# A causal mask as a bank-opening product, and sixteen fp32r warming products, in an mLSTM and feed-forward kernel

## The chip, the cores and the metric

The kernel runs on one core of a Trainium2 chip. The metric is the device time of one execution in microseconds (us), smaller is better. The engines are named as in the profile: PE is TensorE's matrix multiplications and PEld its weight loads, DVE is VectorE, ACT is ScalarE, POOL is GpSimd, and SP issues most of the DMAs.

## The reference

Two layers follow each other. The first is an mLSTM with 4 batches of 8 heads, 768 steps and a head dimension of 40; the second is a feed-forward layer on 3072 tokens (320 to 2048 to 320) with a leaky activation whose slope differs by channel.

```python
for t in range(S):
    m_new = max(f[t] + m, i[t])
    C = exp(f[t] + m - m_new) * C + exp(i[t] - m_new) * outer(v[t], k[t])
    n = exp(f[t] + m - m_new) * n + exp(i[t] - m_new) * k[t]
    y[t] = sigmoid(o[t]) * (C @ q[t]) / max(abs(n . q[t]), 1)
    m = m_new
x = y as (tokens, heads * dim)
h = x @ w_in
out = (max(h, 0) + alpha * min(h, 0)) @ w_out
```

## The kernel before

**Chunks.** The recurrence is computed in chunks of 128 steps, six to a batch, 24 in all, each with all 8 heads. For a chunk `n` and a parity `par` (four heads of even or of odd number), the scores `pS` are products of keys and queries in one PSUM bank of 128 x 512. They are multiplied by a decay matrix `E`: row `s`, column `t` holds exp(L[t] + b[s]), where `L` is the running sum of the log forget gates and `b` a bias of each source step. `E` must be zero where `t < s`; that is the causal mask.

**How `E` is made.** For chunks 0 to 3 PE spreads the row `L` over 128 partitions into a bank `pb`, by four products of 128 columns (one a head): in `spread` for chunks 0 and 1 (L898), in `stage_b` for 2 and 3 (L419), where `LP` holds the sums in three bf16 parts. For later chunks a DMA brings the spread rows (`Lb`). ScalarE takes the exponential with `b` as its bias (L909, L425). Then GpSimd's `affine_select` writes zeros where `t < s` (L913, L429). VectorE multiplies scores and `E` (L933, L447), and PE multiplies the result with the values (`pH`, L311).

**The feed-forward layer.** Tokens are taken in 12 groups of 256 (two chunks). Each operand is split into a high and a low part in fp32r, so that the first layer has 8 products of 256 columns for each of 16 blocks (L593 to L600) and the second 6 of 320 columns (L623). Weights come as 64-bit words; ScalarE and VectorE convert and split them during the first 100 us (L696, L708, L710, L718, L722). Group 1 starts while group 0 is still running.

**What sets the order.** The start, up to the transposed tokens of group 0, is pinned: each name in the string `ORDER` is a step, emitted in that order, and on every engine each instruction is chained to the one before. `sp`, `ex`, `ms`, `sc` and `wg` with a chunk and a parity are the spread, the exponential, the mask, the scores and their multiplication; `l3a` to `l3e` split the sums of chunk 1; `lf`, `li`, `bj`, `wt`, `wd` are gate arithmetic; `u0m` and `u0c` are the state's products and copy; `warmN` are N products of 256 bf16 columns into an unused bank `o0`, which keep PE running. After it the scheduler places instructions by its own estimates, as far as dependences allow. `FILL` gives warming products ahead of the values of chunks 3 to 5. Banks for attention alternate between two tags (`psa`).

Of the kernel before, what the change touches and what calls it, by code (L numbers as in the profile page):

```python
# [17 lines left out]
def kernel(ctx: ExitStack, tc: tile.TileContext, q, k, v, i_gate, f_gate, o_gate, w_in, w_out, alpha, out):  # L18
    nc = tc.nc
    B, H, S, D = q.shape  # L20
    DM, DFF = w_in.shape
    P = 128
    BH = B * H
    NC = S // P
    NPR = H // 2
    GC = 2
# [15 lines left out]
    def psa(name):  # L42
        turns.reverse()
        return ps_a.tile([P, 512], F32, tag=turns[0], name=name)
# [40 lines left out]

    LP = const.tile([3 * BH, GT], BF16, tag="LP", name="LP")
    pick = const.tile([3 * BH, BH], BF16, tag="pick", name="pick")

    def load_qk(n):
        b, c = divmod(n, NC)  # L90
# [317 lines left out]
    def stage_b(n):  # L408

        b, c = divmod(n, NC)  # L410
        Lb, (Q, K, qf) = pre.pop(n), chunk.pop(n)
        Es = []
        for par in range(2):
            E = sb.tile([P, 512], F32, tag="E", name=f"E{n}_{par}", bufs=4)
            if Lb is None:
                pb = psa(f"pb{n}_{par}")
                for p in range(NPR):
                    h = 2 * p + par
                    nc.tensor.matmul(  # L419
                        pb[:, p * P : (p + 1) * P], pick[:, h : h + 1].broadcast_to([3 * BH, P]),  # L420
                        LP[:, n % GC * P : (n % GC + 1) * P], start=True, stop=True,
                    )
            for p in range(NPR):
                h = 2 * p + par
                nc.scalar.activation(  # L425
                    E[:, p * P : (p + 1) * P], Lb[:, h] if Lb is not None else pb[:, p * P : (p + 1) * P], AF.Exp,
                    bias=bT[:, c, b * H + h : b * H + h + 1],
                )
            nc.gpsimd.affine_select(  # L429
                out=E, in_=E, pattern=[[0, NPR], [1, P]], base=0, channel_multiplier=-1,  # L430
                compare_op=ALU.is_ge, fill=0.0,
            )
            if c == 0 and par == 1:
                open_gate(b)
            pS = psa(f"pS{n}_{par}")
            for p in range(NPR):
                sl = slice(p * P, (p + 1) * P)
                if n >= NDIR:
                    h = 2 * p + par
                    for s in range(2):  # L440
                        nc.tensor.matmul(  # L441
                            pS[:, sl], K[: 3 * D, s, h], Q[: 3 * D, s, h], start=s == 0, stop=s == 1
                        )
                else:
                    nc.tensor.matmul(pS[:, sl], K[:R, par, sl], qf[:R, sl], start=True, stop=True)
            if n < NBF:
                nc.vector.tensor_tensor(E, pS, E, ALU.mult)  # L447
                Es.append(E)
            else:
                if par == 0:  # L450
                    E3 = late_pool.tile([P, 2, 512], BF16, tag="t", name=f"E3_{n}", bufs=3)
                Es.append(score_parts(pS, E, E3[:, par]))
            yield
        if c > 0:
            *_, T = from_state(n, qf, Q)
        hv = values(n, Es) if n < NBF else values_by_parts(n, Es)
        if c > 0:
            nc.vector.tensor_tensor(T, T, hv, ALU.add)
            hv = T
# [60 lines left out]
    def attention(n0):  # L520
# [44 lines left out]
    V0, V1 = 0, 2  # L565
    FILL = {3: 4, 4: 14, 5: 4}
    ORDER = """dq0 dq1 dw0 dw2 warm24 dv0 dw1 dw4 do1 dw3 do2 scan lf0a lf0b li0 lf0z L0 bj0 qT0 qc0 kT0 kc0 warm12 sp00
        bTt bTc l3a l3b alT l3c l3d warm6 wt0 ex00 sc00 l3e ms00 warm3 sp01 ewj ex01 ms01 sc01 warm3 eeL wg00 wTt eTt
        wTc eTc lf1a lf1b warm3 w0s wg01 sp10 alC ex10 ms10 warm3 sp11 ex11 qT1 w1s kT1 kc1 w0j0 warm4 li1 wd0 w0j1 w2s
        warm12 u0m qc1 u0c v0 w0h w0l w1j0 L1 w2j0 warm2 sc10 w1j1 warm2 w2j1 wd1 wg10 fsm fst sc11 ms11 warm6 dv1 dq3 wg11 og1  # L570
        lpa lpb bj1 dq2 dL dx2 w1h g0r dx0 g0g lpc lpd lpe g0x g0p w1l dx1 v1 x0 warm4 tadd g1r g1g s0a w2h g1x g1p w2l warm12 x1
        s1a s1d warm3 s0d og2"""

# [237 lines left out]
    def first_group():  # L811
# [17 lines left out]
        w = [None] * 5  # L829
# [2 lines left out]


        make_identity(nc, ident)
        for j in range(NQ):
            nc.gpsimd.memset(qn_t[j][:, :, D:], 0.0)
            nc.gpsimd.memset(kn_t[j][:, :, D:], 0.0)
# [51 lines left out]
        def spread(n, par):  # L889

            pb = psa(f"pb{n}_{par}")
            for p in range(NPR):
                h = 2 * p + par
                if n == 0:
                    pick, x = ident[:BH, h : h + 1].broadcast_to([BH, P]), L
                else:
                    pick, x = row[:, h : h + 1].broadcast_to([3 * BH, P]), L3
                nc.tensor.matmul(  # L898
                    pb[:, p * P : (p + 1) * P], pick, x[:, n * P : (n + 1) * P], start=True, stop=True
                )  # L900
            rows[n, par] = pb

# [2 lines left out]
        def decay(n, par):  # L905
            e = sb.tile([P, 512], F32, tag="E", name=f"E{n}_{par}", bufs=4)
            for p in range(NPR):
                h = 2 * p + par
                nc.scalar.activation(  # L909
                    e[:, p * P : (p + 1) * P], rows[n, par][:, p * P : (p + 1) * P], AF.Exp, bias=bT[:, n, h : h + 1]  # L910
                )
            yield
            nc.gpsimd.affine_select(  # L913
                out=e, in_=e, pattern=[[0, NPR], [1, P]], base=0, channel_multiplier=-1,
                compare_op=ALU.is_ge, fill=0.0,
            )
            E[n, par] = e
            yield

# [20 lines left out]
                p2.append(psa("p2_0"))  # L940
            x_by_channel(0, n, p1[0], p2[0])

        junk = ps_o.tile([P, DM], F32, tag="o0", name="warm")

        def warm(n=1):
            dense(junk, n)
# [129 lines left out]
        for n in range(2):  # L1076
            add(f"qT{n} qc{n}", by_channel(n, 0, nc.scalar.copy))
            add(f"kT{n} kc{n}", by_channel(n, 1, nc.scalar.copy))
            for par in range(2):
                steps[f"sp{n}{par}"] = lambda n=n, par=par: spread(n, par)  # L1080
                add(f"ex{n}{par} ms{n}{par}", decay(n, par))
                steps[f"sc{n}{par}"] = lambda n=n, par=par: scores(n, par)
                steps[f"wg{n}{par}"] = lambda n=n, par=par: weigh(n, par)
        for j in range(3):
# [3 lines left out]
            for step in range(2):  # L1088
                steps[f"w{j}j{step}"] = lambda j=j, step=step: w[j].join([step])
        for name in ORDER.split():  # L1090
            if name.startswith("warm"):
                warm(int(name[4:]))
            else:
                steps[name]()
# [113 lines left out]
```

## Time and profile before

| | |
|---|---|
| time, three runs | 497.78 us median, 497.69 to 501.44 |
| span of the profiled execution | 497.0 us (first to last instruction; its own time is not given apart from the runs) |
| busy: PE, VectorE, ScalarE, GpSimd | 479.6, 324.1, 321.4, 305.9 us |
| mean granted clock of TensorE | 0.997 |
| GpSimd's selects, L429 | 44, mean 677 ns |
| GpSimd's selects, L913 | 4, mean 811 ns |
| warming products, L137 | 107, mean 306 ns |

The span is the time of one execution from its first to its last instruction; some 0.7 us lie around it if it is like the lowest run. In the tables of stretches of time, the columns after the length are busy time (and instructions) of PE, PEld, DVE, ACT and POOL, then the granted clock, the share of busy DMA engines and GB/s. In a timeline, a row is its start, its length, the engine, the line, the operation, output and inputs, shapes and count; what stands in brackets is how long the engine sat idle before it, and what it waited for. [...]

### The profile page before, as it was taken

The numbers are of one execution on the slowest core, as the hardware profiler recorded it, in microseconds if no ns is written. First come the engines' busy times: TensorE is split into PE (matmuls) and PEld (weight loads), VectorE is DVE, ScalarE is ACT, GpSimd is POOL, SyncE is SP. The second block draws the span as 40 slices with busy tenths as digits, with TensorE's granted clock in tenths as the row PEclk, the third lists the DMA queues.
The fourth block names the chain that finished last, engine by engine and source line by source line (L and its number), as shares of the span: only waits on it lengthen the run. The fifth ranks groups of instructions, "written<-read, shape, count | busy, mean of one in ns | idle before, by whom it ended". The sixth has DMA issues, their size and how long they took to land.

```text
span 497.0 us, 11890 instructions
## 1 busy us (share of the span) xinstructions
PE 479.6 (97%) x4509; PEld 458.3 (92%) x4509; DVE 324.1 (65%) x676; ACT 321.4 (65%) x700; POOL 305.9 (62%) x393
## 2 busy tenths in 40 slices
PE   8998889999999999999999999999999999999997
PEld 7877879899998999999899999989999999999997
DVE  7889899945668675675495576666586675642321
ACT  3869498555687776776975677677886663343332
POOL 6542163405559989849498789758888855243242
PEclk9999998999999999999999999999999999999999
DMA  9998977354685577587566675667664230000000
GB/s 171 232 167 235 248 192 216 94 94 96 150 183 118 125 171 160 105 191 151 111 148 131 147 134 123 157 166 139 134 171 76 46 90 1 1 28 1 26 1 26
DMA packets 173922, 61.60 MB, mean 124 GB/s; under 512 B 140154, under 2 KB 166122, under 8 KB 173866
## 3 DMA queue, kind: packets, MB, share of 16 engines
q1 hardware_dynamic: 173786, 60.75, 54.9%
q8 instruction: 35, 0.57, 0.5%
q14 instruction: 21, 0.17, 0.1%
q10 hardware_dynamic: 80, 0.11, 0.1%
HBM read 36.90 MB, written 4.03 MB: 82 GB/s over the span
## 4 chain that ended last, share of the span: by engine, by line
PE 64%; DVE 10%; ACT 8%; POOL 6%; DMA 5%; issue 5%; SPq 1%; ACTq 0%; DVEq 0%; POOLq 0%
PE po L623 25%; PE ph L593 4%; PE ph L596 3%; PE ph L594 3%; PE ph L597 3%; PE ph L599 3%; PE ph L595 3%; PE ph L600 3%; PE ph L598 3%; PE pH L347 2%; PE pS L441 2%; POOL gl L615 2%; PE warm L137 2%; DMA kS<-Z 2%; DMA qS<-Z 1%
## 5 line engine op out<-in xcount | busy, mean ns | idle before, releaser
L615 POOL TENSOR_TENSOR gl<-g,gh 128x512 fp32r<-128x512 f32 x80 | 102.8, 1286 | 62.0 <-ACT gh L614 54.7
L606 DVE SCALAR_TENSOR_TENSOR g<-g,oma,ph 128x256 f32<-128x256 f32 x160 | 69.8, 477 | 74.4 <-ACT g L602 68.8
L623 PE MATMUL po<-OH,gh 128*128 128x320 f32 x368 | 111.1, 314 | 0.6 <-ACT gh L614 0.6
L623 PE MATMUL po<-OL,gh 128*128 128x320 f32 x368 | 109.4, 310 | 0.0
L602 ACT ACTIVATE g<-ph 128x512 f32<-128x512 f32 x96 | 57.1, 595 | 41.0 <-PE ph L600 29.1
L614 ACT CAST gh<-g 128x512 fp32r<-128x512 f32 x80 | 49.5, 619 | 34.4 <-DVE g L606 33.0
L623 PE MATMUL po<-OH,gl 128*128 128x320 f32 x368 | 71.1, 315 | 0.2 <-POOL gl L615 0.2
L623 PEld LDWEIGHTS po<-OH,gh 128*128 128x128 f32 x368 | 69.0, 188 | 1.0 <-ACT gh L614 0.8
L623 PEld LDWEIGHTS po<-OL,gh 128*128 128x128 f32 x368 | 69.0, 188 | 0.0
L593 PE MATMUL ph<-XH,WH 128*128 128x256 f32 x192 | 58.1, 303 | 1.8 <-DVE g L606 0.8
L623 PEld LDWEIGHTS po<-OH,gl 128*128 128x128 f32 x368 | 56.8, 188 | 0.4 <-POOL gl L615 0.4
L425 ACT ACTIVATE E<-Lb,bT 128x128 f32<-128x128 f32 x160 | 51.0, 393 | 7.2 <-PE pH L347 7.1
L429 POOL TENSOR_SCALAR_AFFINE_SELECT E<-E 128x512 f32<-128x512 f32 x44 | 29.8, 677 | 40.7 <-ACT E L425 37.7
L597 PE MATMUL ph<-X,W 128*128 128x256 f32 x192 | 54.5, 285 | 0.0
L594 PE MATMUL ph<-XH,WH 128*128 128x256 f32 x192 | 54.3, 283 | 0.0
L596 PE MATMUL ph<-XH,WL 128*128 128x256 f32 x192 | 54.1, 282 | 0.0
L600 PE MATMUL ph<-X2L,W 128*128 128x256 f32 x192 | 54.0, 282 | 0.0
L599 PE MATMUL ph<-XL,WH 128*128 128x256 f32 x192 | 53.9, 281 | 0.0
L595 PE MATMUL ph<-XH,WL 128*128 128x256 f32 x192 | 53.7, 280 | 0.0
L598 PE MATMUL ph<-XL,WH 128*128 128x256 f32 x192 | 53.5, 279 | 0.0
L334 ACT CAST E<-pS 128x512 bf16<-128x512 f32 x72 | 41.8, 585 | 12.8 <-DVE pS L332 9.0
L593 PEld LDWEIGHTS ph<-XH,WH 128*128 128x128 f32 x192 | 36.2, 188 | 2.9 <-issue 1.0
(199 smaller groups left out, 1154.6 us busy)
## 6 DMA issues: line engine op xcount, KB each, us to landing
Lb<-L_d SPq DMA_DIRECT2D x20, 512.0 KB
wo<-in_moe_w_out_dram SPq DMA_DIRECT2D x8, 640.0 KB
wi<-in_moe_w_in_dram SPq DMA_DIRECT2D x8, 512.0 KB
qn<-in_q_dram SPq DMA_DIRECT2D x24, 160.0 KB
kn<-in_k_dram SPq DMA_DIRECT2D x24, 160.0 KB
va<-in_v_dram SPq DMA_DIRECT2D x24, 160.0 KB
og<-in_o_gate_dram SPq DMA_DIRECT2D x24, 160.0 KB
out_dram<-ob SPq DMA_DIRECT2D x11, 320.0 KB
```

What stands on the lines that cost most here:

```text
L593: nc.tensor.matmul(dst, WH[half][:, 0, hs], XH[:, 0], start=True, stop=False)
L594: nc.tensor.matmul(dst, WH[half][:, 1, hs], XH[:, 1], start=False, stop=False)
L595: nc.tensor.matmul(dst, WL[half][:, 0, hs], XH[:, 0], start=False, stop=False)
L596: nc.tensor.matmul(dst, WL[half][:, 1, hs], XH[:, 1], start=False, stop=False)
L597: nc.tensor.matmul(dst, W2[:, fs], X2, start=False, stop=False)
L598: nc.tensor.matmul(dst, WH[half][:, 0, hs], XL[:, 0], start=False, stop=False)
L599: nc.tensor.matmul(dst, WH[half][:, 1, hs], XL[:, 1], start=False, stop=False)
L600: nc.tensor.matmul(dst, W2[:, fs], X2L, start=False, stop=True)
L602: nc.scalar.activation(gt, ph, AF.Relu, scale=-1.0)
L606: nc.vector.scalar_tensor_tensor(out=y[:, e], in0=gt[:, e], scalar=oma[:, f : f + 1], in1=ph[:, e], op0=ALU.mult, op1=ALU.add)
L615: (nc.vector if g < 2 else nc.gpsimd).tensor_tensor(gl, y, gh.bitcast(F32), ALU.subtract)
L623: nc.tensor.matmul(po[j], x[:, e, j * P : (j + 1) * P], W[f // NB][:, f % NB], **ends)
```

## The change

For chunks 0 to 3, a product now opens the bank `pb`: the matrix `later`, 0 where `t >= s` and -2^100 elsewhere, multiplied with an identity in bf16 and repeated for the four heads. The four products of the spread add to it. The exponential of -2^100 is zero, so GpSimd's select is left out for these chunks. `later` is made by GpSimd at the start, by a memset and a select, ahead of the other memsets. In `ORDER` the four `ms` steps go, and one `warm12` becomes `wide`: sixteen fp32r products of 512, 256, 320 and 128 columns, four each, into the unused bank. Their operand is a tile `even` of 128 x 512, which VectorE writes by one cast from the identity at the start.

```diff
+    later = const.tile([P, P], BF16, tag="later", name="later")
+    def barred(pb):
+        one = ident.bitcast(BF16).rearrange("p (c w) -> p c w", w=2)[:, :, 1]
+        nc.tensor.matmul(pb, one, later.unsqueeze(1).broadcast_to([P, NPR, P]), start=True, stop=False)
...
@@ stage_b
                 pb = psa(f"pb{n}_{par}")
+                barred(pb)
                 for p in range(NPR):
...
-                        LP[:, n % GC * P : (n % GC + 1) * P], start=True, stop=True,
+                        LP[:, n % GC * P : (n % GC + 1) * P], start=False, stop=p == NPR - 1,
...
-            nc.gpsimd.affine_select(
-                out=E, in_=E, pattern=[[0, NPR], [1, P]], base=0, channel_multiplier=-1,
-                compare_op=ALU.is_ge, fill=0.0,
-            )
+            if Lb is not None:
+                nc.gpsimd.affine_select(
+                    out=E, in_=E, pattern=[[0, NPR], [1, P]], base=0, channel_multiplier=-1,
+                    compare_op=ALU.is_ge, fill=0.0,
+                )
...
@@ ORDER
-        bTt bTc l3a l3b alT l3c l3d warm6 wt0 ex00 sc00 l3e ms00 warm3 sp01 ewj ex01 ms01 sc01 warm3 eeL wg00 wTt eTt
-        wTc eTc lf1a lf1b warm3 w0s wg01 sp10 alC ex10 ms10 warm3 sp11 ex11 qT1 w1s kT1 kc1 w0j0 warm4 li1 wd0 w0j1 w2s
-        warm12 u0m qc1 u0c v0 w0h w0l w1j0 L1 w2j0 warm2 sc10 w1j1 warm2 w2j1 wd1 wg10 fsm fst sc11 ms11 warm6 dv1 dq3 wg11 og1
+        bTt bTc l3a l3b alT l3c l3d warm6 wt0 ex00 sc00 l3e warm3 sp01 ewj ex01 sc01 warm3 eeL wg00 wTt eTt
+        wTc eTc lf1a lf1b warm3 w0s wg01 sp10 alC ex10 warm3 sp11 ex11 qT1 w1s kT1 kc1 w0j0 warm4 li1 wd0 w0j1 w2s
+        wide u0m qc1 u0c v0 w0h w0l w1j0 L1 w2j0 warm2 sc10 w1j1 warm2 w2j1 wd1 wg10 fsm fst sc11 warm6 dv1 dq3 wg11 og1
...
         make_identity(nc, ident)
+        nc.gpsimd.memset(later, 0.0)
+        nc.gpsimd.affine_select(
+            out=later, in_=later, pattern=[[1, P]], base=0, channel_multiplier=-1, compare_op=ALU.is_ge, fill=-(2.0**100)
+        )
...
@@ spread
             pb = psa(f"pb{n}_{par}")
+            barred(pb)
...
-                    pb[:, p * P : (p + 1) * P], pick, x[:, n * P : (n + 1) * P], start=True, stop=True
+                    pb[:, p * P : (p + 1) * P], pick, x[:, n * P : (n + 1) * P], start=False, stop=p == NPR - 1
...
@@ decay
-            yield
-            nc.gpsimd.affine_select(
-                out=e, in_=e, pattern=[[0, NPR], [1, P]], base=0, channel_multiplier=-1,
-                compare_op=ALU.is_ge, fill=0.0,
-            )
             E[n, par] = e
...
-        junk = ps_o.tile([P, DM], F32, tag="o0", name="warm")
+        junk = ps_o.tile([P, 512], F32, tag="o0", name="warm")
+        even = late_pool.tile([P, 512], F32R, tag="gh", name="even", bufs=3)
+        nc.vector.tensor_copy(even.rearrange("p (a b) -> p a b", b=P), ident.unsqueeze(1).broadcast_to([P, 4, P]))
+
+        def wide():
+            for cols in (512, 256, 320, 128):
+                for _ in range(4):
+                    nc.tensor.matmul(junk[:, :cols], even[:, :P], even[:, :cols], start=True, stop=True)
```

The order of instructions moves at three places on which the prediction rests. The first is PE's queue in the pinned start, from the second spread of chunk 1 (`pb_1`) over its transposed queries and keys (`pqk`) to the first product of the state (`pu`). Before, the two warming rows after `pqk_1` stand sixteen times in a row:

```order
L898 MATMUL pb_1_311<-L_140,row 128x128 x4
L224 MATMUL pqk_0_321<-ident,qn_76 104x128 x4
L224 MATMUL pqk_1_328<-ident,kn_78 104x128 x4
L137 LDWEIGHTS ident
L137 MATMUL warm<-ident 128x256
L167 MATMUL pu_358<-va_79,kd_341 40x42 x8
```

Now the bank-opening product stands ahead of the spread, and the two warming rows stand four times ahead of the wide ones:

```order
L93 LDWEIGHTS ident
L93 MATMUL pb_1_318<-later,ident 128x512
L911 MATMUL pb_1_318<-L_147,row 128x128 x4
L230 MATMUL pqk_0_329<-ident,qn_76 104x128 x4
L230 MATMUL pqk_1_336<-ident,kn_78 104x128 x4
L143 LDWEIGHTS ident
L143 MATMUL warm<-ident 128x256
L958 MATMUL warm<-even 128x512 x4
L958 MATMUL warm<-even 128x256 x4
L958 MATMUL warm<-even 128x320 x4
L958 MATMUL warm<-even 128x128 x4
L173 MATMUL pu_370<-va_79,kd_349 40x42 x8
```

The same kind of pair stands ahead of the other three spreads of chunks 0 and 1, at the head of what the exponentials wait for. The second place is the head of VectorE's queue, before:

```order
L848 CAST row<-ident 32x32 x3
L849 CAST pick<-row 96x32
L973 SCALAR_TENSOR_TENSOR g_WL_95<-g_WH_94 32x768
L976 TENSOR_TENSOR g_lf_138<-g_WH_94,g_WL_95 32x256
L979 TENSOR_TENSOR g_lf_138<-g_lf_138,g_WL_95 32x256
```

and now:

```order
L860 CAST row<-ident 32x32 x3
L861 CAST pick<-row 96x32
L953 CAST even<-ident 128x512
L988 SCALAR_TENSOR_TENSOR g_WL_96<-g_WH_95 32x768
L991 TENSOR_TENSOR g_lf_145<-g_WH_95,g_WL_96 32x256
L994 TENSOR_TENSOR g_lf_145<-g_lf_145,g_WL_96 32x256
```

The cast stands ahead of the scan of the running maximum (the row of 32x768), on which all gate arithmetic rests. The third place is GpSimd's queue in the part that the scheduler places, for chunks 3 to 5. `E_0_735` and `E_1_759` are chunk 3, `E_0_831` and `E_1_913` chunk 4, `E_0_1237` and `E_1_1421` chunk 5; `xn_719` holds the tokens of group 1, of chunk 2 and then of chunk 3. Before:

```order
L429 AFFINE_SELECT E_0_735<-E_0_735 128x512
L401 TENSOR_TENSOR xn_719<-T_707,og_181 128x320
L405 COPY xn_719<-xn_719 128x64
L429 AFFINE_SELECT E_1_759<-E_1_759 128x512
L429 AFFINE_SELECT E_0_831<-E_0_831 128x512
L145 TENSOR_TENSOR kd_1638<-kn_77,wT 128x320
L429 AFFINE_SELECT E_1_913<-E_1_913 128x512
L429 AFFINE_SELECT E_0_1237<-E_0_1237 128x512
L401 TENSOR_TENSOR xn_719<-T_798,og_181 128x320
L429 AFFINE_SELECT E_1_1421<-E_1_1421 128x512
L405 COPY xn_719<-xn_719 128x64
L145 TENSOR_TENSOR kd_1866<-kn_78,wT 128x320
```

Now, with `xn_730`, `E_0_842` and `E_1_924` for chunk 4, `E_0_1248` and `E_1_1432` for chunk 5:

```order
L151 TENSOR_TENSOR kd_1649<-kn_77,wT 128x320
L407 TENSOR_TENSOR xn_730<-T_718,og_188 128x320
L437 AFFINE_SELECT E_0_842<-E_0_842 128x512
L411 COPY xn_730<-xn_730 128x64
L437 AFFINE_SELECT E_1_924<-E_1_924 128x512
L437 AFFINE_SELECT E_0_1248<-E_0_1248 128x512
L437 AFFINE_SELECT E_1_1432<-E_1_1432 128x512
L151 TENSOR_TENSOR kd_1877<-kn_78,wT 128x320
L407 TENSOR_TENSOR xn_730<-T_809,og_188 128x320
```

The selects of chunk 3 are gone, and the second `xn` of group 1 stands behind the second select of chunk 5 and behind the product `kd_1877`, where before it stood ahead of both.

More of the change, by code (lines that the diff above doesn't have):

```diff
@@ L1080, in first_group @@
                 steps[f"sp{n}{par}"] = lambda n=n, par=par: spread(n, par)
-                add(f"ex{n}{par} ms{n}{par}", decay(n, par))
+                add(f"ex{n}{par}", decay(n, par))
                 steps[f"sc{n}{par}"] = lambda n=n, par=par: scores(n, par)
@@ L1090, in first_group @@
         for name in ORDER.split():
-            if name.startswith("warm"):
+            if name == "wide":
+                wide()
+            elif name.startswith("warm"):
                 warm(int(name[4:]))
```

## The prediction

> **What bounds the kernel now.** I read the busy shares first, then the slices.
>
> ```profile
> PE 479.6 (97%) x4509; PEld 458.3 (92%) x4509; DVE 324.1 (65%) x676; ACT 321.4 (65%) x700; POOL 305.9 (62%) x393
> ...
> PE   8998889999999999999999999999999999999997
> ...
> ```
>
> PE is busy 479.6 of 497.0 us, and in every slice. GpSimd, from which the change takes work, is busy 62%. But PE's share also counts warming products and products that only run long, so I asked for the stretches.
>
> ```profile
> 20.00:30.00 10.00, 9.53 (x93) 8.74 (x88) 9.45 (x21) 6.02 (x12) 5.18 (x6) 1.00 1.25 179
> 30.00:40.00 10.00, 9.09 (x89) 7.76 (x87) 8.02 (x20) 8.47 (x16) 2.38 (x3) 1.00 0.70 196
> ...
> 70.00:80.00 10.00, 8.20 (x56) 7.00 (x55) 9.79 (x17) 8.78 (x19) 4.18 (x5) 0.83 0.84 226
> 100.00:150.00 50.00, 48.91 (x429) 47.73 (x428) 28.22 (x58) 31.96 (x64) 20.73 (x31) 1.00 0.61 134
> ```
>
> The first busy column is PE, the third VectorE, the fifth GpSimd. From 20 to 100 us VectorE is nearly full and PE waits now and then; from 100 us PE alone is full. By the built order the queues differ from before only up to about 115 us; from there on they are the same. So the end moves by as much as PE's work at about 115 us moves, and the question is the first 100 us. There I read the chain of work that ended last.
>
> ```profile
> 8.97 1.08 PE pb L898 x8
> ...
> 15.41 0.50 PE pb L898 x4
> ...
> 15.93 1.65 ACT E L909 x6
> ...
> 21.56 0.04 DVE WL L722
> ```
>
> Up to 15.9 us the chain is PE's own queue without a gap; then ScalarE; from 21.6 us VectorE, which converts weights. GpSimd's masks are not in it.
>
> **The change, part by part.**
>
> *The masks that go.* Eight selects leave GpSimd, four of the first two chunks and four of chunks 2 and 3.
>
> ```profile
> 12.65 0.69 DVE L933 TENSOR_TENSOR E<-pS,E 128x512 f32<-128x512 f32 x1 [0.53 <-POOL E L913]
> ...
> 14.96 0.23 DVE L868 COPY wT<-ps_gw 128x64 f32<-128x64 f32 x1 [1.61 <-PE ps_gw L864]
> ...
> 65.47 0.69 DVE L447 TENSOR_TENSOR E<-pS,E 128x512 f32<-128x512 f32 x1 [0.58 <-POOL E L429]
> ```
>
> Only two waits end with a mask. The first, 0.53 us, is followed on VectorE by 1.61 us of waiting for PE: it is worth nothing, PE's queue is late next. The second, 0.58 us, lies in the VectorE-bound part: I count all of it, **-0.6 us**, between 0 and that.
>
> *The bank-opening products.* Eight bf16 products of 512 columns come in, each ahead of four products of a spread. The trace has none of 512 columns; the nearest row is the warming product of 256.
>
> ```profile
> 17.36 1.91 PE L137 MATMUL warm<-ident 128*128 128x256 bf16 x16
> ...
> 19.11 0.58 ACT L276 COPY kf<-pqk 40x512 f32<-40x512 f32 x1
> ...
> 19.70 0.51 PE L167 MATMUL pu<-va,kd 128*40 128x42 f32 x16 [0.43 <-ACT kf L276]
> ```
>
> Sixteen take 1.91 us; less 0.27 for the last one's own length that is 0.109 us each, so 0.22 us for 512 columns; nothing where PE waits anyway, 0.27 at most. The first stands where PE waits for VectorE's sums (next part) and is hidden. The next three lie in PE's gapless queue: 3 x 0.22 = **0.65 us** on PE, and two of them, 0.43, ahead of ScalarE's exponentials. The four of chunks 2 and 3 stand ahead of these waits of PE, which take them in; without that cover they cost 0.9 us.
>
> ```profile
> PE pb L419 <- ACT qf L284: 1.0, 1, 1.0
> PE ph L593 <- DVE gl L615: 0.7, 1, 0.7
> PE pS L445 <- ACT E L425: 0.7, 1, 0.7
> ```
>
> *The wide warming products.* Sixteen fp32r products of 512, 256, 320 and 128 columns replace twelve of the bf16 ones, 12 x 0.109 = 1.31 us. Their paces are in the feed-forward and in the spread of chunk 1.
>
> ```profile
> 487.79 0.28 PE L598 MATMUL ph<-XL,WH 128*128 128x256 f32 x1
> ...
> 488.14 0.32 PE L623 MATMUL po<-OH,gh 128*128 128x320 f32 x1
> ...
> 489.17 0.31 PE L623 MATMUL po<-OL,gh 128*128 128x320 f32 x1
> ```
>
> Three products of 256 columns start from 487.79 to 488.14, one every 0.117 us, and seven of 320 from there to 489.17, one every 0.147. 512 columns are two of 256, 0.233; 128 are 0.125 (the spread at 15.41, four in 0.50), or 0.06 if half the width takes half the time. Four of each: 4 x (0.233 + 0.117 + 0.147 + 0.125) = 2.49 us, at least 2.2. The swap adds **1.18 us**. The product behind them waited 0.43 us for a copy on ScalarE, which is cover for that much.
>
> *The tile of the wide products.* VectorE writes it by one cast, in front of the long scan with which the start begins.
>
> ```profile
> 1.41 3.33 DVE L848 CAST row<-ident 32x32 fp32r<-32x32 f32 x3 [0.48 <-POOL ident masks.py:199]
> 4.77 0.54 DVE L849 CAST pick<-row 96x32 bf16<-96x32 f32 x1
> 4.86 1.74 DVE L973 TENSOR_TENSOR_SCAN g_WL<-g_WH 32x768 f32<-32x768 f32 x1
> ...
> 5.89 0.52 POOL L268 MEMSET kf<- 64x512 f32 x1
> ...
> 8.90 0.96 PEld L898 LDWEIGHTS pb<-g_L,ident 32*128 32x128 f32 x8 [0.21 <-DVE g_L L982]
> ...
> 10.32 0.27 DVE L1006 CAST L<-g_L 32x256 fp32r<-32x256 f32 x1
> ```
>
> A cast of 256 columns takes 0.27 us at 10.3 us, so 512 take 0.5. But beside GpSimd's memsets three casts of 32 columns took 3.33 us, and the one of `pick` 0.54. GpSimd's memsets last until 6.4 us, and later by 0.5 now, since the barrier tile is made ahead of them (as `ident` was, from 0.80 to 1.31 us). So the scan starts between 0.5 and 1.6 us later; I take 1.0. [...]
>
> PE's weight load waited 0.2 us for the sums at 8.90, so the chain moves by 1.0 - 0.2 = 0.8 us (0.3 to 1.4), and the first new product fits into the wait.
>
> *What is late next.* PE reaches the product of 19.70 us 0.8 + 0.65 + 1.18 - 0.43 = 2.2 us later. VectorE copies its result at 20.65 us, behind a slow multiplication:
>
> ```profile
> 16.58 3.02 DVE L145 TENSOR_TENSOR kd<-kn,wT 128x320 f32<-128x320 f32 x1
> ...
> 20.65 0.66 DVE L182 COPY C<-pu 40x168 f32<-40x168 f32 x2
> ...
> 21.56 0.69 DVE L722 TENSOR_TENSOR WL<-t_wi,WH 128x512 fp32r<-128x512 f32 x1 [0.24 <-ACT WH L718]
> ```
>
> If GpSimd's masks of chunk 1 are part of what stretched that multiplication to 3.02 us, it is shorter now, but VectorE then waits for PE. Of the 2.2 us, 0.44 is the copy's slack (the product takes 0.51 and was done at 20.21) and 0.24 the wait at 21.56: **+1.5 us** (0.8 to 2.1) on VectorE where its own full stretch begins. ScalarE, 0.8 + 0.43 late, is earlier than that.
>
> *What moves.* GpSimd's operations on the second half of the gates start right behind the first weights, at about 10 us, beside VectorE's split of the sums; these are needed by PE at 15.4 us and ended at 12.13: 3 us of cover. In the stretch from 45 to 115 us the second token half of group 1 (`xn`) falls behind a mask and a product on GpSimd.
>
> ```profile
> 72.15 1.32 POOL L401 TENSOR_TENSOR xn<-T,og 128x320 f32<-128x320 f32 x1 [1.58 <-DVE og L399]
> 73.43 0.88 POOL L429 TENSOR_SCALAR_AFFINE_SELECT E<-E 128x512 f32<-128x512 f32 x1
> ...
> 74.46 1.30 POOL L145 TENSOR_TENSOR kd<-kn,wT 128x320 f32<-128x320 f32 x1
> ...
> 79.47 0.42 DVE L492 TENSOR_TENSOR X2L<-p,X 128x256 fp32r<-128x256 f32 x1
> ...
> 84.03 0.19 PEld L598 LDWEIGHTS ph<-XL,WH 128*128 128x128 f32 x1
> ```
>
> It would come 0.88 + 1.30 = 2.2 us later. The last piece made from it is done at 79.9 us, and group 1's first product with a low part starts at 84.03: 4 us of cover, so nothing; without it 2.2. SP's queue only exchanges neighbours (a `kn` ahead of a `wo`, an `Lb` ahead of a `wo`, a `va` ahead of an `Lb`).
>
> **Sum:** +1.5 - 0.6 = +0.9 us. The profiled execution spans 497.0 us, and about 0.7 lie around it if it is like the lowest run (497.69); the median is 497.78. So **498.7 us**; by its own terms 498.0 (the start's shift 0.8) to 500.8 (2.1, no mask's wait won, the later bank products uncovered).
>
> **The rivals.**
>
> *The exchanged queues win the waits back.* From 30 to 100 us PE is idle some 7 us (0.91 and 1.80 of them in the two stretches shown), and once its clock is halved:
>
> ```profile
> 72.00:74.00 2.00, 0.85 (x6) 0.49 (x5) 2.00 (x4) 1.95 (x5) 1.85 (x2) 1.00 0.62 92
> ...
> 76.00:78.00 2.00, 2.00 (x12) 1.75 (x11) 1.94 (x4) 1.47 (x3) 0.00 (x0) 0.50 1.11 360
> ```
>
> PE is idle for more than half of 72 to 74 us, and from 75.0 to 78.4 runs at clock 0.50, which costs 1.7 us. If the new order wins half of the idle time, and a third of the halved stretch, the rest of which holds filler, that is 3.5 + 0.6: 498.7 - 4.1 = 494.6. Against it: VectorE is busy 9.79 of 10 there, and its queue holds the same work.
>
> [...]
>
> *The fp32r pace is a state that the wide products set.* The bf16 products start at 256 / 0.109 = 2.35 columns a nanosecond, the fp32r ones at 2.18 in both widths.
>
> ```profile
> L623 PE MATMUL po<-OH,gh 128*128 128x320 f32 x368 | 111.1, 314 | 0.6 <-ACT gh L614 0.6
> ...
> L593 PE MATMUL ph<-XH,WH 128*128 128x256 f32 x192 | 58.1, 303 | 1.8 <-DVE g L606 0.8
> ```
>
> There are three such groups of 368 and eight of 192. If warming in fp32r brought them to the bf16 pace, 1104 products would gain 0.011 us each and 1536 0.008: 24 us, 475. [...] Against the rival: 2640 such products keep PE at this for 400 us, and the pace at their end is still the slow one.
>
> *The change does nothing that can be seen:* every added piece is covered, 497.8.
>
> **Chances.** Forecast 0.60; queues win 0.14 (a quarter of it beyond 1%); half clock 0.10; fp32r pace 0.13; nothing 0.03. One per cent, 5 us, is about what a measurement of this kernel tells from no change. Faster: 0.13 + 0.04 = 0.17. Slower: 0.09 + 0.02 from the forecast's far tail = 0.11. Same: 0.72. The range runs from 493.5, just below the second case, to 502.8, just short of the third; it leaves out the fp32r pace and a few hundredths on each side.
>
> **What would show it.** In the new profile: the scan of 4.86 us starts near 5.9; the first spread's products near 9.8; the sixteen wide products take 2.5 us; the product of 19.70 us starts near 21.9; VectorE's `WL` of 21.56 us near 23; no wait for a mask at 65 us; and the tail, from 115 us to the end, is as long as before. The forecast is wrong if fp32r products step by other than 0.117 and 0.147 us, if clock 0.50 shows up in more or no stretch, or if PE's waits from 30 to 100 us sum to other than 6 to 8 us.

## The result, and the profile after

| | before | after |
|---|---|---|
| median time | 498.06 us (496.94 to 501.44, 10 runs) | 503.95 us (501.09 to 507.85, 10 runs) |
| ratio to before | | 1.0124, 95% interval 1.0101 to 1.0147 |
| span of the profiled execution | 497.0 us | 500.9 us (its time 502.61) |
| mean granted clock over the runs | 0.997 (the 92 runs of before beside the experiments) | 0.989 |

The change costs 1.2%, about 6 us. The forecast was 498.7 us, with a range up to 502.8. Each listed run's time is 1.7 us above its span, so the 0.7 us that the prediction put around the span was 1 us too small: the profiled execution of before took about 498.7, slightly more than its median. Medians, ratios and clocks, here and below, leave out six runs of the experiments that lie over 1.5% above the fastest of their kernel.

The page of after, its first part:

```profile
PE 482.0 (96%) x4521; PEld 461.2 (92%) x4521; DVE 318.7 (64%) x677; ACT 322.3 (64%) x700; POOL 298.8 (60%) x387
```

GpSimd lost 7 us of work and VectorE 5, on engines that are busy for 60 and 64% of the span. The start came out better than forecast, as the timeline of after shows (start, length, engine, line, and in brackets the idle time ahead):

```profile
1.41 0.55 DVE L860 CAST row<-ident 32x32 fp32r<-32x32 f32 x3 [0.49 <-POOL ident masks.py:199]
...
2.08 0.42 DVE L953 CAST even<-ident 128x512 fp32r<-128x512 f32 x1
4.14 1.75 DVE L988 TENSOR_TENSOR_SCAN g_WL<-g_WH 32x768 f32<-32x768 f32 x1 [1.64 <-DMA g_WH<-in_i_gate_dram]
...
16.02 0.48 DVE L151 TENSOR_TENSOR kd<-kn,wT 128x320 f32<-128x320 f32 x1
...
17.87 2.62 PE L958 MATMUL warm<-even 128*128 128x512 f32 x16
20.42 0.51 PE L173 MATMUL pu<-va,kd 128*40 128x42 f32 x16
...
21.68 0.69 DVE L730 TENSOR_TENSOR WL<-t_wi,WH 128x512 fp32r<-128x512 f32 x1
```

The casts are done at 2.5 us and not at 4.9, the scan waits for a DMA instead, and VectorE's `WL` starts 0.12 us later than in before (21.56). At about 100 us PE's feed-forward is 0.2 to 0.7 us ahead of before. Then it loses time at three places, the last two of them far behind the point from which the queues have the order of before. These are the waiting products of before there:

```profile
111.68 0.41 PE L623 MATMUL po<-OH,gg 128*128 128x320 f32 x1 [0.93 <-ACT gg L614]
...
151.29 0.21 PE L347 MATMUL pH<-vb,E 128*128 128x84 bf16 x1 [1.07 <-ACT E L334]
...
330.99 0.36 PE L593 MATMUL ph<-XH,WH 128*128 128x256 f32 x1 [0.83 <-DVE g L606]
```

And these are the ones of after:

```profile
111.94 0.42 PE L631 MATMUL po<-OH,gg 128*128 128x320 f32 x1 [1.88 <-ACT gg L622]
...
151.51 0.21 PE L353 MATMUL pH<-vb,E 128*128 128x126 bf16 x1 [0.92 <-POOL vb L331]
152.80 0.21 PE L353 MATMUL pH<-vb,E 128*128 128x84 bf16 x1 [1.08 <-ACT E L340]
...
333.49 0.55 PE L601 MATMUL ph<-XH,WH 128*128 128x256 f32 x1 [1.99 <-DVE g L614]
```

The waits are longer by 0.95, 0.92 and 1.16 us, and behind the third PE runs at half clock, which it does not do there in before (table of stretches of after; the figure after POOL's busy time is the granted clock):

```profile
330.00:332.00 2.00, 1.50 (x28) 1.16 (x24) 0.00 (x0) 0.88 (x3) 0.85 (x3) 1.00 0.84 268
333.20:336.50 3.30, 3.01 (x14) 3.04 (x15) 2.74 (x9) 1.82 (x5) 3.00 (x5) 0.50 0.77 191
```

PE's work is 0.3 us later than in before at 111.9 us, 1.5 at 152.8, 2.5 at 333.5 and 3.9 behind the half-clock stretch. From there to the end it stays at 3.9, the difference of the two spans. In between, other waits differ by some 0.3 us in all.

**What the three waits have in common.** Each goes back to a transfer that lands late. At 331 us it is a DMA transpose of a chunk's queries (`qS`), which ScalarE's cast of the next chunk waits for (timeline of before, then of after):

```profile
328.62 0.46 ACT L236 CAST Z<-qn 128x320 bf16<-128x320 f32 x1 [1.28 <-DMA qS<-Z]
```

```profile
331.12 0.46 ACT L242 CAST Z<-qn 128x320 bf16<-128x320 f32 x1 [2.43 <-DMA qS<-Z]
```

Its issue to that cast took 3.30 us before and 4.45 after. The list of DMA queues says what lies between. For the whole execution of before, and then of after, it has this line (packets, MB, share) for a program that comes in pieces of 16 KB:

```profile
q8 instruction: 35, 0.57, 0.5%
```

```profile
q8 instruction: 36, 0.59, 0.5%
```

Here is the view of DMAs of after from 327.5 to 331.2 us, 40 slices of 0.09 us:

```profile
GB/s 266 266 222 67 130 174 174 227 213 396 208 111 66 36 30 11 0 0 0 3 8 8 8 11 8 11 8 11 191 291 288 291 291 436 415 332 415 401 401 415
...
q8 instruction: 1, 0.02, 1.6%
...
qS<-Z SPq DMA_TRANSPOSE x1
```

And from 326.2 to 329.9 us in before, around the same transpose:

```profile
GB/s 288 155 155 114 144 191 222 221 230 216 208 199 221 202 210 199 202 236 349 332 330 374 387 387 374 304 387 244 216 376 221 111 89 66 22 22 0 0 0 169
```

By the list of packets, the transpose of after runs from 327.88 to 330.60 us, and one piece of program starts in its middle, at 328.39. The rate falls from 200 to nothing, and the rest of the transpose follows some 1.2 us later. In before the transpose runs from 326.53 to 328.10, without a hole in the rate; the piece starts at 328.90, when it has ended. The output gates' transfer shows the same. From 104.9 to 108.3 us of after, with a piece at 105.2:

```profile
GB/s 215 226 224 421 194 162 134 156 147 164 169 186 181 188 190 194 139 64 55 36 11 11 9 13 15 15 13 15 15 15 15 15 15 15 6 0 0 0 0 0
```

Its last 1.2 us move at 9 to 15 GB/s. I read that as one DMA engine that was held up by the piece and still has its share to move; the views do not tell the engines apart, so that reading is not shown. ScalarE's step for the sigmoid, ahead of the feed-forward's `gg` in its queue, starts with its table load at 108.31 us instead of 106.38. The third piece, at 140.37, lies in a pair of transposes of 139.0 to 142.7 us. ScalarE's next casts wait for these until 143.31, where before they start at 141.80, and its later steps, for which PE waits at 151, are late by as much.

**Why the pieces moved.** On the average 254 to 255 of the trace's instructions of PE lie between two pieces (251 to 252 of them products and weight loads), in every kernel here. That count is why I take the pieces for PE's program. The change adds 8 bank-opening products and 4 warming ones, each with its weight load: 24 instructions. So every piece behind the start is fetched 24 instructions earlier against the work. At the mean pace, 9042 products and weight loads in 500 us, that is an estimated 1.3 us; the piece that starts at 106.57 us in before starts at 105.21 in after.

### The profile page after: what moved, and what is told of

Same layout as the page of the kernel before. It is cut to its first block, busy times and chain, and to the rows that moved or that the text cites. A ratio compares the mean times of both kernels' runs of the same rounds, so it can differ in the third digit from the quotient of the medians.

```text
span 500.9 us, 11912 instructions
## 1 busy us (share of the span) xinstructions
PE 482.0 (96%) x4521; PEld 461.2 (92%) x4521; DVE 318.7 (64%) x677; ACT 322.3 (64%) x700; POOL 298.8 (60%) x387
## 4 chain that ended last, share of the span: by engine, by line
PE 73%; DVE 9%; ACT 6%; DMA 6%; issue 3%; SPq 1%; POOL 1%; ACTq 0%; POOLq 0%; DVEq 0%
PE po L631 29%; PE ph L601 4%; PE ph L605 4%; PE ph L604 4%; PE ph L602 4%; PE ph L607 4%; PE ph L608 4%; PE ph L603 4%; PE ph L606 4%; PE pH L353 3%; PE pS L449 3%; PE warm L143 2%; DMA qS<-Z 2%; DMA wo<-in_moe_w_out_dram 1%; PE pu L173 1%
## 5 line engine op out<-in xcount | busy, mean ns | idle before, releaser
L601 PE MATMUL ph<-XH,WH 128*128 128x256 f32 x192 | 58.3, 304 | 2.2 <-DVE g L614 2.0
L437 POOL TENSOR_SCALAR_AFFINE_SELECT E<-E 128x512 f32<-128x512 f32 x40 | 25.9, 647 | 30.0 <-ACT E L432 25.5
```

What stands on the lines that cost most here:

```text
L601: nc.tensor.matmul(dst, WH[half][:, 0, hs], XH[:, 0], start=True, stop=False)
```

## The experiments

The theories: **A**, the masks' removal gives another order from 45 to 115 us, and that order costs; **B**, the wide products and the longer start cost; **F**, which came up with the first four runs, the place of PE's program fetches costs; **H**, the half-clock stretches make the rest.

### Parts of the change

The first kernel is after with `warm12` in the place of `wide` and no `even`. The second is before with `wide` and `even`. The third and the fourth take the bank-opening products for chunks 0 and 1, or 2 and 3, alone:

```diff
 spread (chunks 0, 1)        third: kept as in after; fourth: as in before
 stage_b (chunks 2, 3)       third: as in before;     fourth: kept as in after
-  ... w2s wide u0m ...
+  ... w2s warm12 u0m ...    first, third and fourth
```

> The whole change except the wide products: twelve bf16 warming products stand in their old place and the tile of their operand is not made. The queues of GpSimd and SP are those of after, word for word; the masks of chunks 0 to 3 are bank-opening products. Theory A (the masks' removal lets the scheduler place the work from 45 to 115 us in another order, above all SP's two values ahead of the output gates, and PE then waits longer at 110, 150 and 331 us): 503 to 505, the waits of PE at 110 and at 331 us stay at 1.9 and 2.0 us. Theory B (the wide fp32r products make the start longer, and all that follows is late): within 1.5 us of before, 497 to 499.5.

> The kernel before with the sixteen wide products and their tile alone; GpSimd masks all chunks as before, and GpSimd, SP and nearly all of ScalarE have the order of before. Theory A: 497 to 500, since the order from 45 to 115 us is the old one (PE's wait at 110 us near 0.9 us, at 331 near 0.8). Theory B: 501 to 504.

> Bank-opening products for chunks 0 and 1 only (the pinned start); chunks 2 and 3 are masked by GpSimd as before, no wide products. Only four selects leave GpSimd, all inside the pinned order; behind the start every queue has the order of before, except some of VectorE's neighbours. Theory A: 497 to 499, the old waits at 110 and 331 us. If the start itself were the cause (theory B in its wider form: the barrier tile, the casts, the bank-opening products at the head): 500 to 504, with the offset against before there by 22 us and kept to the end.

> Bank-opening products for chunks 2 and 3 only; chunks 0 and 1 are masked by GpSimd in the pinned start as before, no wide products. The order of SP, GpSimd and VectorE from 45 to 115 us is close to that of after. Theory A: 502 to 505, with PE's wait at 110 us at 1.5 us or more. Theory B: 497 to 499.5. A third theory (the offset comes from half-clock stretches that fall anywhere, whatever the order): 498 to 503 with the mean clock below 0.994, and no longer wait at 110 us.

| | median us | ratio to before (interval) | instructions of PE more than before |
|---|---|---|---|
| masks without wide products | 504.77 | 1.0122 (1.0096 to 1.0148) | 16 |
| wide products only | 499.65 | 1.0039 (1.0009 to 1.0069) | 8 |
| chunks 0 and 1 only | 498.95 | 1.0015 (0.9994 to 1.0036) | 8 |
| chunks 2 and 3 only | 499.84 | 1.0018 (0.9993 to 1.0044) | 8 |

Theory B falls with the first row: without the wide products the loss is as large. Theory A falls short with the fourth: it has nearly the order of after and loses 1 to 2 us, not 6. (A's longer wait ahead of the feed-forward's second layer is there in its trace, 1.7 us for `gh` at 106.5 us; A's time is not.) The theory of half clock had asked for a mean clock below 0.994 there; it was 0.9955. The two halves of the masks cost 0.15% and 0.18%, neither told from nothing by its interval, and together 1.2%. No theory had forecast that, and it sent me to the traces of DMAs. The waits of PE in the first kernel:

```profile
PE ph L601 <- DVE g L614: 2.6, 2, 2.2
...
PE pH L143 <- DVE E L455: 2.1, 1, 2.1
```

and in the fourth:

```profile
PE pH L354 <- ACT E L341: 2.3, 2, 1.2
PE pH L144 <- DVE E L456: 2.1, 1, 2.1
...
PE ph L602 <- DVE g L615: 0.8, 1, 0.8
```

Both have the new wait of 2.1 us ahead of chunk 4's values. Only the first has the long wait for `g`, 2.2 us at 336 us, and its trace has a piece of program at 331.46 us inside that transpose. But the first kernel does not lose its time where after does. The wait near 110 us that theory A named for it is not there. PE is 3.3 us behind before at 100 us already. Just ahead of that lie waits of 1.6 and 1.3 us, and 10.24 us at half clock (a row of its table of stretches):

```profile
87.60:97.90 10.30, 9.35 (x53) 8.79 (x54) 7.62 (x16) 4.87 (x13) 3.12 (x4) 0.50 0.14 24
```

### The place of the fetches alone

To shift the fetches and nothing else, warming products of the start are joined in pairs to one of 512 columns (2 instructions fewer for each pair), or halved (2 more). The columns that PE passes stay the same, and so does the order on every other engine:

```diff
         def warm(n=1):
+            x = ident.bitcast(BF16)
+            while n >= 2 and merged[0] > 0:
+                nc.tensor.matmul(junk, x[:, :P], x.unsqueeze(1).broadcast_to([P, 2, 2 * P]), start=True, stop=True)
+                merged[0] -= 1
+                n -= 2
             dense(junk, n)
```

> The changed kernel with 8 of its first 24 warming products joined in pairs to four of 512 columns: the same columns, but 4 products and 4 weight loads fewer in PE's program. Theory F (PE's program is fetched in pieces of 16 KB by a DMA that shares the engines of the data; the change put 24 instructions more into PE's queue, so each fetch comes about 1.5 us earlier against the work, and three of them now hit transfers that PE waits for: the output gates at 105, a transpose at 140, one at 328 us): 8 instructions are too few. The fetches come near 105.6, 140.9 and 328.9 us, all three transfers are still hit, PE's waits near 110, 150 and 331 us stay at 1.9, 0.9 and 2.0 us, and the time is that of after, 502.5 to 505. Theory A (the order of the queues alone): 502.5 to 505 as well. It is the control for the next one.

> The same with 32 products joined to sixteen: 32 instructions fewer than after, 8 fewer than before, the order of every other queue that of after. Theory F: the fetches come near 106.8, 141.7 and 329.9 us, behind the three transfers; PE's waits near 110, 150 and 331 us fall to about 0.9, 0 to 0.3 and 0.8 us, no half clock behind 331 us: 4 to 5 us less than after, 498.5 to 500.5. Theory A: as after, 502.5 to 505.

> The same with 64 products joined to thirty-two: 64 instructions fewer than after. Theory F: the fetches come near 108, 142 and 330.3 us, clear of the three transfers by more; 498 to 501. A gain over the kernel with sixteen pairs would speak for the joined products themselves. Theory A: as after, 502.5 to 505.

> The kernel before with 28 of its warming products at the start split into two of 128 columns each: the same columns, 56 instructions more in PE's program, no other queue changed and no mask moved. Theory F: the fetch of 106.57 us comes near 103.8, into the output gates' transfer, that of 141.3 near 139, into a transpose, and that of 328.9 near 326.9, into the transpose of the queries: PE's waits near 110, 150 and 330 us grow by about 1 us each, with a half-clock stretch behind the last: 501 to 503.5. Theory A, and any theory by which the masks or the wide products are the cause: as before, 497.5 to 499.

| | instructions against before | median us | ratio to before (interval) |
|---|---|---|---|
| after, 4 pairs joined | +16 | 503.6 | 1.0128 (1.0088 to 1.0168) |
| after, 16 pairs joined | -8 | 500.29 | 1.0038 (1.0018 to 1.0058) |
| after, 32 pairs joined | -40 | 502.68 | 1.0114 (1.0073 to 1.0156) |
| before, 28 products halved | +56 | 505.94 | 1.0171 (1.0134 to 1.0207) |

In its profiled run, which took 497.29 us and was the fastest of its twelve, the kernel with sixteen pairs has the three waits back at their old length or below:

```profile
109.44 0.41 PE L631 MATMUL po<-OH,gg 128*128 128x320 f32 x1 [0.62 <-ACT gg L622]
...
149.81 0.21 PE L353 MATMUL pH<-vb,E 128*128 128x84 bf16 x1 [1.03 <-ACT E L340]
...
329.56 0.36 PE L601 MATMUL ph<-XH,WH 128*128 128x256 f32 x1 [0.83 <-DVE g L614]
```

The control with four pairs kept two of them in its profile (1.6 us for `gg`, 2.2 for `g`) and the loss. And before itself, its masks untouched, becomes slower by 1.7% when 56 instructions are added that leave PE the same columns to pass:

```profile
114.99 0.42 PE L623 MATMUL po<-OH,gg 128*128 128x320 f32 x1 [1.81 <-ACT gg L614]
...
156.29 0.21 PE L347 MATMUL pH<-vb,E 128*128 128x126 bf16 x1 [0.93 <-POOL vb L325]
157.59 0.21 PE L347 MATMUL pH<-vb,E 128*128 128x84 bf16 x1 [1.08 <-ACT E L334]
...
340.59 0.36 PE L593 MATMUL ph<-XH,WH 128*128 128x256 f32 x1 [1.58 <-DVE g L606]
```

The first three rows are those of after, in a kernel without the change. It lost more than I forecast, since its pieces hit other transfers too: one starts at 55.9 us, ScalarE waits 3.2 us for a weight of the second layer (2.4 in before), PE then 2.2 us for ScalarE's `qf` (1.0 in before), and 6.83 us at half clock follow.

The kernel with 32 pairs missed its forecast of 498 to 501. Its waits for `gg` and `g` are 0.6 and 0.8 us, as forecast, but its pieces lie elsewhere: one at 58.3 us beside a weight (PE waits 1.5 us for `qf`), one at 136.3 in a pair of transposes (1.4 us for `XH`), and its profile, the slowest of its five runs (507.17 us), is at half clock twice between 62 and 90 us, for 10.24 us each time. These shifts did not end the hits, they exchanged them.

### Both kernels at both places

> The kernel before with 12 of its first warming products split into two of 128 columns each: 24 instructions more in PE's queue, as many as the change adds; no mask moved, no other queue changed. Theory F (where PE's program is fetched decides): the fetches come 1 to 1.5 us earlier against the work; they hit the output gates' transfer near 105.2 us and a transpose near 140.9, and miss the one of 326 us by a little unless the work is late by then. PE's wait near 110 us grows to 1.5 to 2 us and one near 150 comes in: 500 to 503. If the cause lies in the masks and in the order of the queues, with the fetches only adding to it: 497 to 499.

> The changed kernel with its 24 first warming products joined to twelve: PE's queue is as long again as before, all other queues are those of after. Theory F: the fetches stand where they stood before, so the time is within 2 us of before, 497.5 to 500.5, like the kernel with sixteen pairs joined. If the new order of the queues costs by itself, more than that: 501 to 504.

> The changed kernel with 44 products joined to 22: 20 instructions fewer than before. Counted on the traces, a shift of this size leaves only 4 of the fetches behind 115 us in a transpose (as in before) and none in the output gates' transfer, where the kernel with sixteen pairs still has one. Theory F: 497 to 499.5, lower than with sixteen pairs by up to 1.5. If what is left over before (2 to 3 us with sixteen pairs) is the new order or the wide products and not the fetches: 499.5 to 501.

> The masks' part of the change alone (no wide products), with 36 warming products joined to 18: again 20 instructions fewer than before. Theory F: 496.5 to 499, against 504.8 for the same kernel without the joining. It would tell the wide products apart: if these cost time by themselves, it is 1 to 2 us below the kernel with 22 pairs; if not, the same. If the masks' new order is what costs: 502 to 505.

| | fetches as in before | 24 instructions earlier |
|---|---|---|
| before | 1 | 1.0053 (1.0022 to 1.0084), 499.86 us |
| after | 1.0026 (0.9999 to 1.0053), 499.75 us | 1.0124 (1.0101 to 1.0147), 503.95 us |

With the fetches at their old place the change is just not told from no change, though its median is 2.2 us above that of before beside it (497.58); moving the fetches costs before 0.5% and after 1.0%. The kernel before with 24 instructions more came in under its forecast of 500 to 503, and two of the three hits that I had named for it did not come: at 111 us PE waits 0.8 us, and there is no new wait at 151. Its transfers stand elsewhere against PE's work. In its profiled run, one of the longer ones (502.9 us), a piece hit the transpose of 328 us, and this wait is the 2.1 us here; whether the piece missed it in the shorter runs, down to 497.4, is not shown.

```profile
PE ph L593 <- DVE g L606: 2.8, 2, 2.1
```

The two kernels at -20 instructions missed: 501.04 us with the wide products (1.0052, 1.0026 to 1.0077), 503.31 for the masks only (1.0111, 1.0074 to 1.0147), where I had forecast 497 to 499.5 and 496.5 to 499. I had counted the hits on the trace of another kernel. In theirs a piece starts at 130.6 and at 132.9 us in a pair of transposes, as in the kernel with 32 pairs, and PE waits 1.0 and 1.3 us behind it. That is a small part of 3.5 and 5.7 us. Each profile also has 10.24 us at half clock: from 74.3 us, behind a wait of 2.1 us, and from 88.8, behind waits of 1.5 and 1.3. The 503.31 lies in the range that I had set down for the new order as the cause, 502 to 505. So for the masks alone, moving the fetches was not shown to win anything (ratios 1.0122 and 1.0111): their place accounts for the loss of after, and not for that of every kernel with these masks. The masks-only kernel is not below the one with wide products, so the wide products were not shown to cost anything.

A count over all sixteen traces speaks for the fetches all the same. A piece starts at a transpose (from 0.5 us ahead of its first packet to 1.3 us behind it) twice in before and five times in after. In the seven kernels with two such hits, four of them with the new order, the medians lie between 497.3 and 500.3 us. In the nine with three to five, two of them with the old order, they lie between 499.9 and 505.9. It is a count of one profiled run each, not every hit makes PE wait, and what a kernel loses ahead of its first transpose, near 119 us, is not in it.

### The rest

With twelve pairs joined the median is still 2.2 us above before, at a mean clock of 0.9917 against 0.9977 in the runs beside it. A fit to the 78 runs of before, after and the first four kernels, with a base for each kernel, gives 0.33 us for each 0.001 of mean clock: 6.0 x 0.33 = 2.0 us. So the rest has the size of the half-clock stretches. They follow longer waits of PE (table of stretches of this kernel):

```profile
70.00:74.00 4.00, 1.52 (x13) 1.10 (x11) 3.97 (x10) 3.94 (x10) 1.36 (x2) 1.00 0.74 147
85.50:89.20 3.70, 1.74 (x16) 1.54 (x15) 3.70 (x9) 2.92 (x6) 1.81 (x3) 0.99 0.49 147
89.20:92.50 3.30, 3.30 (x15) 3.30 (x15) 3.30 (x7) 1.89 (x3) 2.19 (x2) 0.50 0.02 5
```

Two waits of 2 us for VectorE's product of scores and decays stand where before had several short ones. Behind the first nothing happened in this run, behind the second the clock was halved; in after it was the first. The last two kernels were to tell more. One leaves out the fourteen warming products ahead of chunk 4's values, the other has the fourth kernel's masks with four pairs joined:

```diff
-    FILL = {3: 4, 4: 14, 5: 4}
+    FILL = {3: 4, 5: 4}
```

> The changed kernel without the fourteen warming products ahead of chunk 4's values (1.69 us of PE at full clock, behind PE's wait of 2.09 us at 72 us), which also puts PE's later program fetches, from 72 us on, within 4 instructions of where they stood before. Theory F: no hit in the output gates' transfer or at 328 us any more, so 498 to 500.5 instead of 504. If the rest is half-clock stretches (theory H), leaving the filler out makes PE emptier there: the mean clock stays at 0.992 or falls, and the time is 499 to 501.5. If the rest is PE work and order, the 1.5 us of filler come back in full: 496.5 to 498.5 at a mean clock like before's, 0.996 or more.

> Bank-opening products for chunks 2 and 3 only, with 8 warming products joined to four, so that PE's queue is as long as before; the new order from 45 to 115 us stays. Without the joining this kernel took 499.9 us, at a mean clock of 0.9945. Theory F with H: the long wait of 2.09 us at 70 us stays, so the mean clock stays between 0.991 and 0.996, 498.5 to 500. If all of its distance from before was the shift of the fetches by 8 instructions: 497 to 498.3, at 0.997.

Without the filler: 502.45 us, 1.0100 (1.0062 to 1.0137), outside the 498 to 500.5 of theory F. The waits for `gg` and `g` are short, as theory F wants, but the mean clock of its five runs fell to 0.987 and PE was at half clock twice in its profile, for 6.83 us each time:

```profile
74.00:80.00 6.00, 6.00 (x30) 6.00 (x30) 5.87 (x10) 5.01 (x13) 2.69 (x4) 0.50 0.75 247
86.00:90.50 4.50, 1.81 (x12) 1.35 (x10) 3.71 (x6) 3.85 (x7) 2.34 (x3) 0.99 0.01 3
90.50:97.00 6.50, 6.31 (x28) 6.16 (x28) 4.11 (x9) 1.18 (x2) 0.78 (x1) 0.50 0.01 3
```

The 1.5 us of filler did not come back; more was lost than with twelve pairs joined, which speaks for H, though its size (1 us above the end I gave) was not forecast, and this kernel's order differs a little too. Chunks 2 and 3 alone, matched: 498.88 us, 1.0023 (1.0002 to 1.0044), mean clock 0.994, inside what F with H forecast. Matching won nothing against 1.0018 without it: these 8 instructions were not what it lost by. That the rest is the clock alone is thus argued by its size and by these two, not shown: no run held the order and took the half-clock stretches away. No version beat before.

## Why the prediction was wrong, by its own steps

**The step that failed** is "from there on they are the same. So the end moves by as much as PE's work at about 115 us moves". The queues are the same and PE's work at 111.9 us had moved by 0.3 us, less than the 0.9 forecast; the end moved by 3.9 in the profiled run and by 6 in the median. The same order did not give the same waits with the pieces of program elsewhere against it: the third wait is 1.99 us in after and 0.83 in before. The prediction counted the new products by their time on PE, and not as instructions: the place of the fetches was put at nothing, without a reason. Taking the 24 instructions out again, with all other queues as in after, brings the distance from before down from 5.9 to 2.2 us, each against the runs of before beside it: 3.7 us of the 6, and 4.9 by the two ratios. With 32 instructions taken out the distance is 2.7 us, with 8 it is still 6.0. That the length of PE's queue is the cause is shown by these three kernels. That it acts through the held-up transfers is read from the traces.

**Half clock.** The case "half clock" (0.10 in the chances, put at 503.3 us, just above the range) is what came: behind the third wait, and between 62 and 99 us in most kernels that share the new order. In after's profile there are two stretches, at 73.7 and at 333.1 us, where before has one, at 75.0, each of them at a clock of 0.50 for 3.41 us. How little work of PE halves the clock is not shown: in after PE is busy for 1.62 us of the 3.50 from 108.5 us and for 1.50 of the 3.50 from 149.5, and the clock stays at 1.00 there and in the 3.5 us behind each. By the fit, the share of the clock in the 6 us is (0.9975 - 0.9891) x 330 = 2.8 us; it overlaps with the part above, since some stretches follow a hit. In the traces the stretches that the end does not cut short last 3.41, 6.83 or 10.24 us. The same kernel differs from run to run: the ten runs of after have mean clocks from 0.983 to 0.993.

**The start: the cast of `even` had the wrong sign.** It was to delay the scan by 1.0 us; the scan starts 0.7 earlier. GpSimd's memset and select of `later` (0.20 and 0.33 us, from 1.32) stand where its first memsets stood, the three casts of 3.33 us take 0.55, and `even` itself 0.42. In the kernel with the wide products alone, where GpSimd's queue is the old one, the three casts take 3.33 us again, `even` takes 0.71 and the scan starts at 5.50, 0.6 us later than in before: so the sign came with `later`, and the delay was near its lower end. The cast of `even` in after ran its 0.42 us from 2.08, and the memset of `kn` beside it took 0.60 us instead of 0.26: there it was the memset that ran long, where in before it had been the casts. The other terms of the start came out close: the first spread's products start 0.5 us earlier than in before (8.50 against 8.97) where they were to be 0.8 later, and the product `pu` 0.7 later where it was to be 2.2.

**What held.** The sixteen wide products took 2.62 us, the length of the last one included (2.49 forecast). The multiplication `kd` takes 0.48 us where it took 3.02, and VectorE then waits 3.87 us for PE, as the prediction held possible. It takes 0.48 in the kernel with chunks 0 and 1 alone too, and 3.03 in the two that keep their masks. No wait for a mask is left at 65 us. The fp32r pace is unchanged, so that rival is out; nine starts near the end of after, of which these are the first and the last two ahead of a group:

```profile
492.02 0.32 PE L631 MATMUL po<-OH,gh 128*128 128x320 f32 x1
...
493.05 0.31 PE L631 MATMUL po<-OL,gh 128*128 128x320 f32 x1
493.20 0.75 PE L631 MATMUL po<-OH,gl 128*128 128x320 f32 x4
```

Eight steps in 1.18 us are 0.147 each, less than half of the 0.31 us that one product lasts in the trace, so they overlap. The new order's lead on VectorE, 1 to 3 us between 65 and 110 us, was hardly won on PE, as the prediction said against the rival of the exchanged queues: PE's idle time from 30 to 100 us is 6.4 us, against 7.1 in before.

## What to carry to other kernels

In this kernel, which PE bounds over some 9000 instructions, 24 more of them moved every later fetch of PE's program, by an estimated 1.3 us; in before this alone cost 0.5%, and 56 more cost 1.7%. So a change that looks neutral or good can lose a per cent to transfers that are then hit, and a second one can seem to win by moving them back: with sixteen pairs joined, after went from 1.0124 to 1.0038. Before a small difference is put down to a change, run it once more with PE's queue made as long as it was, by joining or halving products that do nothing. A better place could not be chosen from another kernel's trace: four of my shifts hit new transfers.

## What the runs showed of the hardware that I had not expected

- What I take for PE's program, by the 254 to 255 instructions to a piece, comes by DMA in pieces of 16 KB, 35 or 36 in 500 us, each 0.88 to 1.91 us long (sixteen traces). The sixteen traces hold 576 transposes of 1024 packets of 256 bytes. In 52 of them a piece started from 0.5 us ahead to 1.3 us behind the first packet, and 44 of these took 2.2 us or more. Of the other 524, the median is 1.43 us and 29 took as long as 2.2.
- At the three places of after a hit cost PE about 1 us of waiting each. Behind the third its clock was halved, and PE fell back by 1.4 us more against before in the stretch from 333.1 to 336.5 us.
- How much of a run is at half clock differs between runs of one kernel: the mean clocks of after's ten runs go from 0.983 to 0.993, of the kernel with twelve pairs from 0.988 to 0.999, and their times over 6.8 and 4.2 us. So medians of ten runs and their mean clock are needed to see 2 us.
